# Last two products of a row-tile block set moved beside the next batch's products, one block sum a step, chunk 14 computed plainly

## The chip, the cores and the metric

The kernel runs on one NeuronCore of a Trainium2 chip. The metric is the device time of one execution in microseconds (us). Its engines are named as the profile names them: PE (TensorE, the matmuls), PEld (its weight loads), DVE (VectorE), ACT (ScalarE), POOL (GpSimd) and SP, which issues most of the DMAs.

## The reference

```python
attn_out = softmax(causal(q k^T / 8 + min(bias, 0))) v        # 2 x 8 heads, 576 x 64
x = attn_out as [1152, 512]
P = sinkhorn(exp(x @ w_gate), 8 rounds)                       # 1152 x 8
out = sum over e of P[:, e] * (relu(x @ w1[e]) @ w2[e])       # 8 experts, 512 -> 1024 -> 512
h = out @ w_in ; g = softplus(h) ; result = g @ w_out         # 512 -> 2048 -> 512
```

All products keep nearly full float32 precision: each factor is split into a high and a low part, and a product of two blocks is high x high, high x low and low x high, three matmuls for each 128 rows of contraction.

## The kernel before

After the attention, the work is cut into 20 chunks x of 512 hidden columns: chunks 0 to 15 are the eight experts (`NX` = 16, two chunks each), chunks 16 to 19 the last feed-forward (`NH` = 20). A chunk has an up side (x @ w1 with the activation) and a down side (the result @ w2, added to `acc`). Tokens are two batches g of 576 rows, each four row tiles of 128 and half of the fifth, middle tile (`NB` = 4).

**Up side.** `Unit` computes a batch's up side for one of two column halves a, b with a seven-product block scheme, products p1, p2, p6, p7, p5, p3, p4. Each is six matmuls with 288 moving columns (line 502). ACT and DVE evict the results.

**Down side.** Plain: `downs` does for each row tile four steps of three matmuls of 512 columns (line 578) and one DVE addition into `acc`. In the chunks that `SEVEN` lists (14, 17, 18 and 19), `pairs` replaces it: the four row tiles of a batch are two pairs (r = 0, 1), each a 2 x 2 block product done in seven products a11, s3, s2, a22, s1, s4, a12. One product of one pair is six matmuls of 256 columns (line 420) and a DVE addition `add_to` (lines 381, 384); 14 of these make one batch. The middle tile stays plain. The PSUM bank of a pair (`py`) holds all its products one after the other, and a product on a bank waits until the addition of the product before on the same bank has read it.

**What the block scheme needs ahead.** The up side's results go in full precision into `hw` (`evict`, `word`). `h_steps` makes from them the sums s3, s2, s1, s4 (POOL, line 334), the high parts (ACT, line 327) and the low parts (DVE, line 330; `hl`, `sl`; the middle tile's is the one of 128x256, name "m"). `prep_b` and `prep_t` make the blocks of w2 and their sums t1 to t4 for the next chunk (POOL line 256, ACT 243 and 226, DVE 245 and 228). w1's sums and splits are lines 161 to 170 (POOL), 152 (ACT) and 155 (DVE).

**Order.** It is written by hand: `play` walks a string. "a1" and the like are up products, "d" takes one step of the down side, "E", "F", "e" append a batch's block preparation to a list, "x", "y", "=" and "w" others; after each product or d, `step` advances every list by one. A chunk x plays two strings: the A string has the up products of (x, batch 1) beside the down side of (x, batch 0), the B string the up products of (x+1, batch 0) beside the middle tile and the down side of (x, batch 1). Before, the 14 steps of `pairs(x, 0)` all stand in A and those of `pairs(x, 1)`, behind four steps of the middle tile, all in B. After the last up product, the string for chunk 19's second batch has only down steps: the tail.

Of the kernel before, what the change touches and what calls it, by code (L numbers as in the profile page):

```python
# [20 lines left out]
def attention_moe_ffn(ctx, tc, q, k, v, s, w_gate, w1, w2, w_in, w_out, out):  # L21
# [107 lines left out]
    sp_t = {}  # L129
    SEVEN = (NX - 2, NX + 1, NX + 2, NX + 3)  # L130

# [190 lines left out]
    def h_steps(x, g, part):  # L322

        z = h_sets(g)

        def high(n):
            nc.scalar.activation(out=z[n][0], in_=z[n][2], func=AF.Copy)

        def low(n):
            nc.vector.tensor_tensor(out=z[n][1], in0=z[n][2], in1=f(z[n][0]), op=ALU.subtract)  # L330
            ready.add((x, g, n))

        def sum_(o, a, b, op):
            nc.gpsimd.tensor_tensor(out=z[o][2], in0=z[a][2], in1=z[b][2], op=op)

        if part == "e":
            hold((x, g), (None,))
            sum_("s3", "a11", "a21", ALU.subtract)
            high("a11")
            yield  # L340
            low("a11")
            yield
            last = (x - 1 + g, 1 - g)
            assert not seven(last[0]) or (*last, "done") in ready
            high("s3")
            yield
        elif part == "E":
            high("m")
            high("a22")
            yield  # L350
            low("s3")
            low("m")
            low("a22")
            sum_("s2", "a22", "s3", ALU.subtract)
            yield
            sum_("s1", "a21", "a22", ALU.add)
            yield
            high("a12")
            yield
            low("a12")  # L360
            high("s2")
            yield
            sum_("s4", "a12", "s2", ALU.subtract)
            high("s1")
            yield
            low("s2")
            low("s1")
            hold(None, ((x, g),))
            yield
        else:  # L370
            high("s4")
            yield
            low("s4")
            yield

    def add_to(x, t, cols, py, first, tile_col):
# [11 lines left out]

    def pairs(x, g, middle=None):

# [15 lines left out]
        for a, b, bank, start, tile_, col, first in (  # L406
# [4 lines left out]
            if a == "s3" and middle is not None:  # L411
                yield from middle
            for r in range(2):
# [8 lines left out]
                flush()  # L422
                if a == "s4" and r:
                    ready.add((x, g, "done"))
                add_to(x, rows_of(g) // P + 2 * r + tile_, d[col], o, first, (tile_, col))
# [60 lines left out]
    class Unit:  # L486
# [32 lines left out]
        def p2(self):  # L519
# [3 lines left out]
            nc.vector.tensor_tensor(out=b, in0=b, in1=self.v1, op=ALU.add)  # L523
            evict(self.x, 5 if seven(self.x) else 0, b, self.p, self.h0)

# [10 lines left out]
        def p5(self):  # L536
# [4 lines left out]
            defer(0, lambda: nc.vector.tensor_tensor(out=t, in0=self.c, in1=u4, op=ALU.add))  # L541
            evict(self.x, 1, t, self.p + 2, self.h1)

# [59 lines left out]
    with tc.manual_schedule():  # L603
# [685 lines left out]
        def play(seq, todo, d=None):  # L1289


            for z in seq.split():
# [14 lines left out]
                if z[0] in "eEF":  # L1307
                    g = int(z[1])
                    if seven(x if g else x + (z[0] == "e")):
                        side.append(h_steps(x if g else x + (z[0] == "e"), g, z[0]))  # L1310
                    continue
# [30 lines left out]
        for x in range(NH):  # L1342
# [101 lines left out]
```

## Time and profile before

| what | us |
|---|---|
| median of 3 runs (lowest, highest) | 1088.13 (1088.04, 1088.27) |
| profiled execution | 1089.59 |
| its span, first to last instruction | 1087.8 |
| PE busy | 1056.2 (97%) |
| DVE busy | 799.5 (73%) |
| ACT / POOL busy | 525.3 (48%) / 406.1 (37%) |
| granted TensorE clock, mean | 0.996 |

The 1.8 us between span and execution lie outside the instructions. A PE duration in a row is that of one pipelined matmul to its modelled end; what a matmul costs in a dense row is the distance of two starts. A chunk's stretch is read between two like places of neighbouring chunks.

### The profile page before, as it was taken

Reading aid. Unit: us, or ns where it says so; the run is one execution under the profiler, and the core shown is the slowest. Engines: PE = TensorE matmul, PEld = TensorE weight load, DVE = VectorE, ACT = ScalarE, POOL = GpSimd, SP = SyncE. Lnnn points to the kernel's source line nnn. Section 1 sums busy time; section 2 is a strip of 40 time slices with the busy share of each in tenths; the row PEclk is TensorE's granted clock in tenths of the full one; section 3 lists DMA queues with packets and bytes.
Section 4 is the critical chain, followed back from the end, with each engine's and each line's share of the span. In section 5 each row is a group of like instructions: output and inputs, shape, how many; then the busy total and the mean of one; then the engine's idle time right before and its main releaser. Section 6 shows DMA issues by size and latency. Waiting matters only on the chain.

```text
span 1087.8 us, 18435 instructions
## 1 busy us (share of the span) xinstructions
PE 1056.2 (97%) x6876; PEld 942.5 (87%) x6876; DVE 799.5 (73%) x1725; ACT 525.3 (48%) x1232; POOL 406.1 (37%) x449
## 2 busy tenths in 40 slices
PE   6999999999999999999999999999999999999987
PEld 4777888889888888988888898888899888898987
DVE  5576566667877878787887888775477487678876
ACT  6998544334443433434343343334454365555542
POOL 8885303053342414134241423423262233546321
PEclk9999999999999999999999999999999999999999
DMA  6221111122232222223222231311111011201002
GB/s 195 78 83 55 39 40 39 40 92 96 89 130 88 80 97 98 100 77 124 91 74 98 97 107 68 127 59 39 39 40 59 20 40 39 78 21 59 1 16 73
DMA packets 31538, 78.47 MB, mean 72 GB/s; under 512 B 5856, under 2 KB 13024, under 8 KB 31448
## 3 DMA queue, kind: packets, MB, share of 16 engines
q1 hardware_dynamic: 28704, 68.69, 18.9%
q0 software_dynamic: 2560, 8.39, 2.0%
q8 instruction: 54, 0.88, 0.3%
q14 instruction: 36, 0.29, 0.1%
q10 hardware_dynamic: 184, 0.20, 0.1%
HBM read 65.99 MB, written 10.75 MB: 71 GB/s over the span
## 4 chain that ended last, share of the span: by engine, by line
PE 82%; DVE 10%; ACT 3%; issue 2%; POOL 2%; DMA 0%; POOLq 0%; ACTq 0%; DVEq 0%
PE py L578 36%; PE ph L502 35%; PE py L420 5%; DVE hl L330 2%; PE sc L794 2%; POOL eb L857 1%; PE pv L901 1%; DVE sl L330 1%; PE tr L875 1%; DVE xl L1198 1%; DVE acc L381 1%; DVE xt L1229 1%; DVE ph L523 1%; PE sc L798 1%; DVE w1l L155 1%
## 5 line engine op out<-in xcount | busy, mean ns | idle before, releaser
L502 PE MATMUL ph<-xh,w1h 128*128 128x288 f32 x1120 | 331.7, 296 | 0.3 <-ACT v L510 0.3
L502 PE MATMUL ph<-xh,w1l 128*128 128x288 f32 x1120 | 330.8, 295 | 0.0
L502 PE MATMUL ph<-xl,w1h 128*128 128x288 f32 x1120 | 329.3, 294 | 0.0
L578 PE MATMUL py<-w2h,hh 128*128 128x512 f32 x588 | 233.5, 397 | 1.0 <-DVE acc L590 1.0
L578 PE MATMUL py<-w2l,hh 128*128 128x512 f32 x588 | 232.5, 395 | 0.2 <-POOL w2l L201 0.2
L578 PE MATMUL py<-w2h,hl 128*128 128x512 f32 x588 | 232.4, 395 | 0.0
L502 PEld LDWEIGHTS ph<-xh,w1h 128*128 128x128 f32 x1120 | 210.0, 188 | 18.4 <-ACT v L510 0.5
L502 PEld LDWEIGHTS ph<-xl,w1h 128*128 128x128 f32 x1120 | 210.4, 188 | 16.9
L502 PEld LDWEIGHTS ph<-xh,w1l 128*128 128x128 f32 x1120 | 210.3, 188 | 0.0
L510 ACT ACTIVATE v<-ph 128x288 f32<-128x288 f32 x160 | 64.0, 409 | 187.5 <-PE ph L502 184.8
L469 ACT ACTIVATE hh<-ph 128x288 fp32r<-128x288 f32 x180 | 73.7, 411 | 151.8 <-DVE ph L552 78.2
L578 PEld LDWEIGHTS py<-w2h,hl 128*128 128x128 f32 x588 | 110.5, 188 | 26.5
L201 POOL TENSOR_TENSOR w2l<-raw,w2h 128x512 fp32r<-128x512 f32 x36 | 51.3, 1427 | 215.9 <-ACT w2h L199 215.9
L596 DVE SCALAR_TENSOR_TENSOR acc<-py,gate,acc 128x512 f32<-128x512 f32 x118 | 88.0, 746 | 49.2 <-PE py L578 49.0
L1166 POOL TENSOR_TENSOR cm<-cm,ct 128x512 f32<-128x512 f32 x32 | 45.1, 1408 | 201.5 <-DVE ct L1164 201.5
L578 PEld LDWEIGHTS py<-w2h,hh 128*128 128x128 f32 x588 | 110.4, 188 | 10.5 <-DVE acc L590 1.2
L578 PEld LDWEIGHTS py<-w2l,hh 128*128 128x128 f32 x588 | 110.5, 188 | 10.0 <-POOL w2l L201 0.7
L155 DVE TENSOR_TENSOR w1l<-raw,w1h 128x512 fp32r<-128x512 f32 (+1 forms) x160 | 109.8, 686 | 11.3 <-ACT w1h L152 11.3
L476 DVE SCALAR_TENSOR_TENSOR hl<-ph,hh 128x288 fp32r<-128x288 f32 x180 | 81.2, 453 | 26.7 <-ACT hh L469 25.1
L152 ACT ACTIVATE w1h<-raw 128x512 fp32r<-128x512 f32 (+1 forms) x160 | 91.1, 571 | 0.0
L541 DVE TENSOR_TENSOR t<-ph,v 128x288 f32<-128x288 f32 x80 | 36.4, 455 | 54.5 <-ACT v L510 53.9
L510 ACT ACTIVATE u<-ph 128x288 f32<-128x288 f32 x80 | 32.7, 411 | 55.5 <-PE ph L502 53.4
(246 smaller groups left out, 1779.2 us busy)
## 6 DMA issues: line engine op xcount, KB each, us to landing
raw<-in_w SPq DMA_DIRECT2D x64, 512.0 KB
f<-in_w_in SPq DMA_DIRECT2D x16, 512.0 KB
f<-in_w_out SPq DMA_DIRECT2D x16, 512.0 KB
wd<-cm POOLq DMA_DIRECT2D x32, 256.0 KB, 3.1
raw<-wd SPq DMA_DIRECT2D x16, 512.0 KB
vv<-in_v SPq DMA_DIRECT2D x8, 256.0 KB
out<-acc SPq DMA_DIRECT2D x16, 128.0 KB
qk<-in_k SPq DMA_DIRECT2D x7, 288.0 KB
```

The costliest lines, as they stand in the source:

```text
L152: nc.scalar.activation(out=hi[:, o], in_=t[:, src], func=AF.Copy)
L155: nc.vector.tensor_tensor(out=lo[:, o], in0=t[:, src], in1=f(hi[:, o]), op=ALU.subtract)
L201: (nc.gpsimd if i else nc.vector).tensor_tensor(out=lo, in0=t[:, r], in1=f(hi), op=ALU.subtract)
L420: nc.tensor.matmul(o, u, v, start=(start and c == 0 and n == 0), stop=(c == 1 and n == 2), skip_group_check=True)
L469: nc.scalar.activation(out=hh, in_=z, func=AF.Relu)
L476: nc.vector.scalar_tensor_tensor(out=hl, in0=z, scalar=0.0, in1=f(hh), op0=ALU.max, op1=ALU.subtract)
L502: nc.tensor.matmul(o, u, v, start=(start and c == 0 and n == 0), stop=(c == 1 and n == 2), skip_group_check=True)
L510: nc.scalar.activation(out=t, in_=self.a, func=AF.Copy)
L541: defer(0, lambda: nc.vector.tensor_tensor(out=t, in0=self.c, in1=u4, op=ALU.add))
L578: nc.tensor.matmul(py[t], u, v, start=(k == 0 and n == 0), stop=(k == NF - 1 and n == 2))
L596: nc.vector.scalar_tensor_tensor(out=a, in0=py, scalar=gate_t[0][:, t, e:e + 1], in1=a, op0=ALU.mult, op1=ALU.add)
L1166: nc.gpsimd.tensor_tensor(out=m, in0=m, in1=f(t), op=ALU.add)
```

## The change

Four things: chunk 14 leaves `SEVEN`; A and B strings of the block chunks pair every up product with one d (two where the middle tile stands), so that the last four steps of a batch's 14 (s4 and a12, both pairs) fall beside the next batch's a1, b1, a2, b2; `h_steps` makes its sums and splits in 13 steps where it had 3 and 7, starting with the string and no longer before it; the words of p2 and p5 are written later (8 and 4 flushes instead of 5 and 1). In the tail, the last four steps of batch 0 come first and the middle tile's four steps (D) stand between down steps.

```diff
-    SEVEN = (NX - 2, NX + 1, NX + 2, NX + 3)
+    SEVEN = (NX + 1, NX + 2, NX + 3)
...
-        if part == "e":
-            hold((x, g), (None,))
-            sum_("s3", "a11", "a21", ALU.subtract)
-            high("a11")
-            yield
-            low("a11")
-            yield
...
-            high("s3")
-            yield
-        elif part == "E":
-            high("m")
-            high("a22")
-            yield
-            low("s3")
-            low("m")
-            low("a22")
-            sum_("s2", "a22", "s3", ALU.subtract)
-            yield
-            sum_("s1", "a21", "a22", ALU.add)
-            yield
...
+        if part == "F":
+            assert (x, g, "s3 done") in ready
             high("s4")
             yield
             low("s4")
             yield
+            return
+        hold((x, g), (None,))
+        sum_("s3", "a11", "a21", ALU.subtract)
+        high("m")
+        yield
+        high("a11")
+        low("m")
+        yield
+        high("a22")
+        low("a11")
+        yield
+        low("a22")
+        yield
...
+        high("s3")
+        yield
+        low("s3")
+        yield
+        sum_("s2", "a22", "s3", ALU.subtract)
+        yield
+        high("a12")
+        yield
+        sum_("s1", "a21", "a22", ALU.add)
+        yield
+        high("s2")
+        yield
+        low("s2")
+        yield
+        low("a12")
+        high("s1")
+        yield
+        sum_("s4", "a12", "s2", ALU.subtract)
+        low("s1")
+        hold(None, ((x, g),))
+        yield
...
-            evict(self.x, 5 if seven(self.x) else 0, b, self.p, self.h0)
+            evict(self.x, 8 if seven(self.x) else 0, b, self.p, self.h0)
...
-            evict(self.x, 1, t, self.p + 2, self.h1)
+            evict(self.x, 4 if seven(self.x) else 1, t, self.p + 2, self.h1)
...
-        A7_SEQ = "E0 a1 b1 a2 b2 =0 d d a6 d b6 d d F0 a7 d d b7 =1 d d a5 d b5 d d a3 d b3 e1 a4 d b4"
-        A7_LAST = "E0 a1 b1 a2 b2 d a6 d d b6 d d F0 a7 d d b7 d d a5 d b5 d a3 d b3 e1 a4 b4 d d"
-        B7_SEQ = ("E1 a1 b1 =2 a2 b2 d d d d a6 d d {11} b6 d d {3} F1 a7 d b7 d {2} a5 d b5 d {4} d a3 d {1} d b3 e0 d {22} a4 d b4 d {21}")
+        A7_SEQ = ("E0 a1 ~ b1 ~ {22} a2 ~ b2 ~ {21} =0 a6 d b6 d a7 d b7 d F0 =1 a5 d b5 d a3 d b3 d a4 d b4 d")
+        B7_SEQ = ("E1 a1 d b1 d a2 d b2 d =2 a6 d d b6 d d {12} a7 d d {11} b7 d d {3} F1 a5 d b5 d {2} a3 d b3 d {4} a4 d b4 d {1}")
...
+        LAST = "E1 d d D d D d D D d d d d F1 " + "d " * 10
...
+                d = then(d if seven(x - 1) else (), pairs(x, 0))
+                play(seq, products(x, 1), d)
...
+                    d = then(d, downs(x, [(NB,)]), pairs(x, 1))
...
-                    play("E1 n n n n " + "d " * 8 + "F1 " + "d " * 10, {}, pairs(x, 1, downs(x, [(NB,)], "tr")))
+                    middle = downs(x, [(NB,)], "tr")
+                    play(LAST, {"D": lambda: next(middle)}, then(d, pairs(x, 1)))
```

"~" is a d where the chunk before was a block chunk too, and nothing in chunk 17.

**DVE around the middle tile in chunk 17's B string, before.** The row of `acc<-py` with 512 columns is the middle tile's addition; `hl` and `sl` rows are low parts, `w1l` w1's, `ph` rows up products, `acc` with 256 columns one block product's addition:

```order
L381 TENSOR_TENSOR acc<-py,acc 128x256
L330 TENSOR_TENSOR hl<-hw,hh 128x2x2x128
L552 TENSOR_TENSOR ph<-ph,u 128x288
L330 TENSOR_TENSOR sl<-xw,sh 128x512
L330 TENSOR_TENSOR hl<-hw,hh 128x4x64
L330 TENSOR_TENSOR hl<-hw,hh 128x2x2x128
L523 TENSOR_TENSOR ph<-ph,v 128x288 x2
L155 TENSOR_TENSOR w1l_10580<-raw_10106,w1h_10579 128x256
L330 TENSOR_TENSOR hl<-hw,hh 128x2x2x128
L330 TENSOR_TENSOR sl<-xw,sh 128x512
L330 TENSOR_TENSOR hl<-hw,hh 128x2x2x128
L593 TENSOR_TENSOR acc<-py,acc 128x512
```

The same place after:

```order
L330 TENSOR_TENSOR hl<-hw,hh 128x2x2x128
L384 TENSOR_TENSOR acc<-py,acc 128x256
L330 TENSOR_TENSOR hl<-hw,hh 128x2x2x128
L524 TENSOR_TENSOR ph<-ph,v 128x288
L384 TENSOR_TENSOR acc<-py,acc 128x256
L330 TENSOR_TENSOR sl<-xw,sh 128x512
L524 TENSOR_TENSOR ph<-ph,v 128x288
L384 TENSOR_TENSOR acc<-py,acc 128x256
L155 TENSOR_TENSOR w1l_10463<-raw_9972,w1h_10462 128x256
L330 TENSOR_TENSOR sl<-xw,sh 128x512
L330 TENSOR_TENSOR hl<-hw,hh 128x2x2x128 x2
L594 TENSOR_TENSOR acc<-py,acc 128x512
```

The additions of s4 and a12 of the batch before now stand between the low parts; the four rows right ahead of the middle tile's addition are the same work as before.

**DVE in the tail, before,** from the last up products (L552) to the middle tile's addition (`pyt`):

```order
L552 TENSOR_TENSOR ph<-ph,u 128x288 x2
L330 TENSOR_TENSOR hl<-hw,hh 128x2x2x128
L381 TENSOR_TENSOR acc<-py,acc 128x256 x2
L330 TENSOR_TENSOR sl<-xw,sh 128x512
L330 TENSOR_TENSOR hl<-hw,hh 128x4x64
L330 TENSOR_TENSOR hl<-hw,hh 128x2x2x128
L381 TENSOR_TENSOR acc<-py,acc 128x256
L330 TENSOR_TENSOR hl<-hw,hh 128x2x2x128
L381 TENSOR_TENSOR acc<-py,acc 128x256
L330 TENSOR_TENSOR sl<-xw,sh 128x512
L330 TENSOR_TENSOR hl<-hw,hh 128x2x2x128
L593 TENSOR_TENSOR acc<-pyt,acc 128x512
```

The same place after:

```order
L553 TENSOR_TENSOR ph<-ph,u 128x288
L384 TENSOR_TENSOR acc<-py,acc 128x256 x3
L330 TENSOR_TENSOR hl<-hw,hh 128x4x64
L330 TENSOR_TENSOR hl<-hw,hh 128x2x2x128
L384 TENSOR_TENSOR acc<-py,acc 128x256
L330 TENSOR_TENSOR hl<-hw,hh 128x2x2x128
L384 TENSOR_TENSOR acc<-py,acc 128x256
L330 TENSOR_TENSOR sl<-xw,sh 128x512
L594 TENSOR_TENSOR acc<-pyt,acc 128x512
L384 TENSOR_TENSOR acc<-py,acc 128x256 x3
L330 TENSOR_TENSOR sl<-xw,sh 128x512
```

The middle tile's low part (128x4x64) now stands behind three additions, and the low parts of a12, s2 and s1 no longer stand ahead of the middle tile's addition.

## Rows read from the trace of the kernel before

**Rows 1.** Stretches: us, busy of PE, PEld, DVE, ACT, POOL, clock, DMA.

```profile
734.16:781.64 47.48, 47.48 (x277) 42.56 (x277) 24.73 (x48) 18.49 (x43) 12.25 (x13) 1.00 0.13 45
953.84:1004.11 50.27, 46.33 (x350) 44.60 (x350) 42.12 (x74) 27.19 (x60) 24.38 (x21) 1.00 0.13 43
1004.11:1054.58 50.47, 46.32 (x350) 44.63 (x350) 42.03 (x73) 26.27 (x58) 20.77 (x17) 1.00 0.00 1
```

**Rows 2.** Timeline of PE, chunk 17: start, duration, first matmuls of five steps.

```profile
961.02 0.29 PE L502 MATMUL ph<-xh,w1h 128*128 128x288 f32 x1
...
961.82 0.28 PE L420 MATMUL py<-w2h,hh 128*128 128x256 f32 x1
...
962.52 0.29 PE L502 MATMUL ph<-xh,w1h 128*128 128x288 f32 x1
...
968.80 0.39 PE L578 MATMUL py<-w2h,hh 128*128 128x512 f32 x1
...
970.20 0.39 PE L578 MATMUL py<-w2h,hh 128*128 128x512 f32 x1
```

**Rows 3.** PE's waits from 940 to 1065 us: total, times, longest.

```profile
PE py L420 <- DVE acc L381: 6.0, 9, 1.1
PE py L420 <- DVE acc L593: 2.7, 2, 1.3
PE py L420 <- ACT w1h L152: 1.1, 1, 1.1
```

**Rows 4.** Pieces of the chain that ended last, chunks 13 and 15.

```profile
748.32 1.40 PE py L578 x6
...
845.23 1.40 PE py L578 x6
```

**Rows 5.** Timeline around the middle tile's addition in chunk 17.

```profile
971.73 1.67 POOL L334 TENSOR_TENSOR hw<-hw,xw 128x512 f32<-128x512 f32 x1 [0.96 <-DVE hl L330]
...
972.18 1.78 DVE L330 TENSOR_TENSOR hl<-hw,hh 128x512 fp32r<-128x512 f32 x1
...
973.88 0.68 DVE L593 TENSOR_TENSOR acc<-py,acc 128x512 f32<-128x512 f32 x1
...
974.61 0.39 PE L420 MATMUL py<-w2h,hh 128*128 128x256 f32 x1 [1.34 <-DVE acc L593]
```

**Rows 6.** Timeline around the low part of t3 in chunk 17.

```profile
982.49 1.73 POOL L256 TENSOR_TENSOR xw<-raw,raw 128x512 f32<-128x512 f32 x1
...
983.33 1.43 DVE L245 TENSOR_TENSOR tl<-raw,th 128x512 fp32r<-128x512 f32 x1
...
985.05 0.41 DVE L381 TENSOR_TENSOR acc<-py,acc 128x256 f32<-128x256 f32 x1
...
985.52 0.38 PE L420 MATMUL py<-th,hh 128*128 128x256 f32 x1 [1.08 <-DVE acc L381]
```

**Rows 7.** Groups of 953.84 to 1054.58: count, busy us, mean ns, idle before.

```profile
L381 DVE TENSOR_TENSOR acc<-py,acc 128x256 f32<-128x256 f32 x56 | 23.0, 417 | 7.7 <-PE py L420 7.4
L330 DVE TENSOR_TENSOR hl<-hw,hh 128x512 fp32r<-128x512 f32 x16 | 16.5, 1033 | 0.0
```

```profile
L334 POOL TENSOR_TENSOR xw<-hw,xw 128x512 f32<-128x512 f32 x4 | 5.3, 1324 | 10.7 <-ACT hh L327 7.1 <-DVE sl L330 3.7
...
L168 POOL TENSOR_TENSOR raw<-raw 128x256 f32<-128x256 f32 x4 | 2.9, 737 | 1.4 <-DVE w1l L155 1.4
```

**Rows 8.** One low part with no POOL work beside it, chunk 17.

```profile
965.35 0.68 DVE L330 TENSOR_TENSOR hl<-hw,hh 128x512 fp32r<-128x512 f32 x1
```

**Rows 9.** The tail: timeline of PE, then a stretch with its clock.

```profile
1064.92 0.28 PE L420 MATMUL py<-w2h,hh 128*128 128x256 f32 x1
...
1075.16 0.36 PE L420 MATMUL py<-th,sh 128*128 128x256 f32 x1 [2.23 <-DVE acc L381]
...
1084.04 0.28 PE L420 MATMUL py<-w2h,hl 128*128 128x256 f32 x1
```

```profile
1076.60:1080.00 3.40, 3.40 (x18) 3.40 (x18) 1.87 (x4) 0.00 (x0) 0.00 (x0) 0.51 0.11 38
```

More of the change, by code (lines that the diff above doesn't have):

```diff
@@ L334, in sum_ @@
             nc.gpsimd.tensor_tensor(out=z[o][2], in0=z[a][2], in1=z[b][2], op=op)
-        if part == "e":
-            hold((x, g), (None,))
-            sum_("s3", "a11", "a21", ALU.subtract)
-            high("a11")
-            yield
-            low("a11")
-            yield
-            last = (x - 1 + g, 1 - g)
-            assert not seven(last[0]) or (*last, "done") in ready
-            high("s3")
-            yield
-        elif part == "E":
-            high("m")
-            high("a22")
-            yield
-            low("s3")
-            low("m")
-            low("a22")
-            sum_("s2", "a22", "s3", ALU.subtract)
-            yield
-            sum_("s1", "a21", "a22", ALU.add)
-            yield
[L358 to L370, printed above, removed]
+        if part == "F":
+            assert (x, g, "s3 done") in ready
             high("s4")
@@ L374, in h_steps @@
             yield
+            return
[11 more added lines that the diff above has]
+        yield
+        last = (x - 1 + g, 1 - g)
+        assert not seven(last[0]) or (*last, "s4 done") in ready
+        high("s3")
[19 more added lines that the diff above has]
+        yield
     def add_to(x, t, cols, py, first, tile_col):
@@ L387, in add_to, with pairs @@
             nc.sync.dma_start(out=out[t * P:(t + 1) * P, cols], in_=a)
-    def pairs(x, g, middle=None):
+    def pairs(x, g):
         z = h_sets(g)
@@ L410, in pairs @@
                 ("a12", "b21", 1, True, 0, 0, False)):
-            if a == "s3" and middle is not None:
-                yield from middle
             for r in range(2):
@@ L422, in pairs @@
                 flush()
-                if a == "s4" and r:
-                    ready.add((x, g, "done"))
+                if r:
+                    ready.add((x, g, a + " done"))
                 add_to(x, rows_of(g) // P + 2 * r + tile_, d[col], o, first, (tile_, col))
@@ L1306, in play @@
                     continue
[L1307 to L1310, printed above, removed]
+                if z[0] in "EF":
+                    side.append(h_steps(x, int(z[1]), z[0]))
+                    continue
+                if z[0] == "X":
+                    bot.append(prep_b(x, z[1:]))
                     continue
@@ L1323, in attention_moe_ffn @@
         TURN = ("t0 d d d d u0 d d d d d a1 d b1 d a2 d =2 b2 t1 d a6 d b6 d a7 d b7 d a5 d b5 d d u1 w0 a3 w2 b3 w1 a4 w3 b4")
-        A7_SEQ = "E0 a1 b1 a2 b2 =0 d d a6 d b6 d d F0 a7 d d b7 =1 d d a5 d b5 d d a3 d b3 e1 a4 d b4"
-        A7_LAST = "E0 a1 b1 a2 b2 d a6 d d b6 d d F0 a7 d d b7 d d a5 d b5 d a3 d b3 e1 a4 b4 d d"
-        B7_SEQ = ("E1 a1 b1 =2 a2 b2 d d d d a6 d d {11} b6 d d {3} F1 a7 d b7 d {2} a5 d b5 d {4} d a3 d {1} d b3 e0 d {22} a4 d b4 d {21}")
-        TO_SEVEN = B_SEQ.replace("b2", "b2 y3 y2 y4 y1").replace("b3", "b3 e0")
-        B7 = {True: {"11": "x11 x12 y0", "3": "y3", "2": "y2", "4": "y4", "1": "y1", "22": "x22", "21": "x21"},
-              False: {"11": "w0 w1", "3": "", "2": "", "4": "", "1": "", "22": "", "21": "w2 w3"}}
+        A7_SEQ = ("E0 a1 ~ b1 ~ {22} a2 ~ b2 ~ {21} =0 a6 d b6 d a7 d b7 d F0 =1 a5 d b5 d a3 d b3 d a4 d b4 d")
+        B7_SEQ = ("E1 a1 d b1 d a2 d b2 d =2 a6 d d b6 d d {12} a7 d d {11} b7 d d {3} F1 a5 d b5 d {2} a3 d b3 d {4} a4 d b4 d {1}")
+        TO_SEVEN = B_SEQ.replace("b2", "b2 y3 y2 y4 y1")
+        B7 = {True: {"12": "x12", "11": "x11 y0", "3": "y3", "2": "y2", "4": "y4", "1": "y1"},
+              False: {"12": "", "11": "w0 w1", "3": "", "2": "", "4": "", "1": "d d d d w2 w3"}}
+        A7 = {True: {"~": "d", "{22}": "X22", "{21}": "X21"}, False: {"~": "", "{22}": "", "{21}": ""}}
+        LAST = "E1 d d D d D d D D d d d d F1 " + "d " * 10
         A_GROUPS = [(0, 1), (2,), (3,)]
@@ L1351, in attention_moe_ffn @@
             if seven(x):
-                play(A7_SEQ if x + 1 < NH else A7_LAST, products(x, 1), pairs(x, 0))
+                seq = A7_SEQ
+                for k, z in A7[seven(x - 1)].items():
+                    seq = seq.replace(k, z)
+                d = then(d if seven(x - 1) else (), pairs(x, 0))
+                play(seq, products(x, 1), d)
             else:
@@ L1366, in attention_moe_ffn @@
                         seq = seq.replace("{" + k + "}", z)
-                    play(seq, products(x + 1, 0), then(downs(x, [(NB,)]), pairs(x, 1)))
+                    play(seq, products(x + 1, 0), d)
                 else:
-                    play("E1 n n n n " + "d " * 8 + "F1 " + "d " * 10, {}, pairs(x, 1, downs(x, [(NB,)], "tr")))
+                    middle = downs(x, [(NB,)], "tr")
+                    play(LAST, {"D": lambda: next(middle)}, then(d, pairs(x, 1)))
                 if not seven(x + 1):
```

## The prediction

> **What bounds the kernel now.** I read the stretches first [rows 1]: in a plain chunk PE is busy for all of its 47.48 us, so nothing but matmuls sets the pace there. In a block chunk PE is idle: 50.27 and 50.47 us for fewer columns. The timeline of PE gives the prices [rows 2]: an up product (six matmuls of 288) takes 961.82 - 961.02 = 0.80 us, a block step (six of 256) 962.52 - 961.82 = 0.70, three of 512 (970.20 - 968.80) / 2 = 0.70. A block chunk has 28 up products, 28 block steps and 4 middle steps: 28 x 0.80 + 32 x 0.70 = 44.8 us. So 5.5 us of each block period are no matmul work. The list of PE's waits says what ended them [rows 3]: between 940 and 1065 us twelve waits, 6.0 + 2.7 + 1.1 = 9.8 us, nearly all for a DVE addition. The list counts from the modelled end of a matmul of 0.28 us, while the next would have started after 0.12, so each wait costs 0.16 more: 9.8 + 12 x 0.16 = 11.7 us. The tail has one of 2.2 [rows 9].
>
> Why DVE is late is seen in two places. Around the middle tile [rows 5] a low part starts at 972.18 and takes 1.78 us; alone such a row takes 0.68 [rows 8]. It ends 0.56 us after the POOL sum that runs from 971.73 to 973.40. So it stood still until POOL had finished. Behind it, at 973.88, comes the middle tile's addition, and PE, whose bank it frees, resumes at 974.61. At t3 [rows 6] it is the same: the POOL sum ends at 984.22, the low part at 984.76, and the addition that PE waits for starts at 985.05. Over two periods the low parts of 512 average 1033 ns, the additions, which read PSUM and one tile in SBUF, 417 [rows 7]. DVE is therefore not full (42.1 of 50.3 us [rows 1]); it is an in-order queue in which additions stand behind low parts that POOL holds up.
>
> **The change, part by part.**
> Chunk 14 plain. From a place in chunk 13 to the same place in chunk 15 the chain takes 845.23 - 748.32 = 96.91 us [rows 4]; two plain chunks take 94.96 [rows 1]. Chunk 14 costs 1.95 us more as blocks than plain, although it saves 12 matmuls of 512 (2.8 us): its stalls and the rest eat that and more. Plain, it is one more of a kind that keeps PE busy throughout [rows 1]. Gain **1.95 us**; its preparation on POOL, DVE and ACT goes with it at no further price, since PE sets the pace.
>
> Strings of chunks 17 to 19. Matmuls are the same in number. What moves is the distance between two products on one bank: before, in "d d a6 d d", a bank's next product came 0.70 to 1.50 us after the last (one block step, with or without an up product); now there is an up product, the other pair's step and an up product between them, 0.80 + 0.70 + 0.80 = 2.30 us, except in the four places of B with two d in a row, 1.50 us. An addition needs some 0.16 for the last matmul's end and 0.42 [rows 7], so DVE may now lag by about 1.7 us, or 0.9, before PE stops. No wait is added; the additions of s4 and a12 are now queued beside the first low parts of the next batch. I take each kind of stall in turn, with 0.6 us of DVE time for a low part alone and the rest of the POOL sum where one has just started.
> - Middle tile (2 x 1.5 us): the same four DVE rows stand ahead of its addition, but its last matmul now comes about 10.4 us into the string instead of 6.0, while the low parts start where they did. They are through by 10.2, the addition ends at 11.2, its bank is wanted at 11.9. Kept: 0.
> - t3's low part (1.6 us in each of two B strings: the wait of 1.08 in [rows 6] with its 0.16, and a small one ahead of it): t3 still needs two POOL sums on w2's raw blocks, which wait for the low parts of these blocks, some 15 us into the string, and its low part then meets the third sum. s2's addition for the second pair is queued behind it: wanted at 20.1 us, done at about 21.5. Kept: 1.4 each, 2.8 in all; bounds 0 and 1.6 each.
> - A strings (the rest of the 11.7, 5.5 us in three strings): the sums s2 and s1 and four of w1's meet low parts of w2, s2, a12, s1 and w1 on DVE; each takes a POOL sum of 0.7 to 1.3 us [rows 7] and 0.57 of its own, five of them some 7 us, and four additions 1.4, against 7 us of PE from the first of them to the bank that they block. Chunk 18 keeps 1.0; chunk 17, where w1's sums come earlier, 0.4; chunk 19, which has none, 0.3. Kept: 1.7; bounds 0 and 5.5.
> So 11.7 us fall to 4.5: gain **7.2 us**, bounds 11.7 and 3.0 (all of t3 and A kept).
>
> The block sums spread over 13 steps cost nothing by themselves: each has the same POOL, ACT and DVE work. The product s3 comes 9.8 us into an A string, in chunk 17 7.0, and its sum and parts take some 1.3, 0.6 and 0.6 of it, so I put nothing on the head start that is gone. The later words hold p2's bank until the seventh product, where nothing asks for it.
>
> Tail. From the last up product's end, 1064.92, to the last matmul, 1084.04 + 0.12, are 19.24 us [rows 9] for 16 block steps and 4 middle steps: 14.1. Excess 5.1: the wait of 2.2 with its 0.16, two small ones of 0.65, 15 matmuls at a granted clock of 0.51 (from 1076.60 on, after PE had done almost nothing from 1072.9 to 1075.16), 0.21 instead of 0.12 each, 1.4 in all, and some 0.5 of a bank chain too tight at 0.70. After, there are two more block steps here and two fewer before. The first middle step starts 1.4 us in and wants the middle tile's low part, which stands behind s4's second addition: done at 2.4, so 0.5 lost. Later a12's and s1's low parts stand between additions with s4's POOL sum beside them: 1.2 lost at a22; the chain at the end 0.3. Kept 2.0, gain **3.1 us**; bounds 4.6 (only the chain is kept) and 1.5 (the low clock comes back). No wait there reaches the 2.2 us that came before the low clock; after the 1.34 us wait [rows 5] the clock stayed at 1.00 through the stretch [rows 1].
>
> Sum: 1.95 + 7.2 + 3.1 = 12.2 us. The profiled execution, 1089.59 (span 1087.8 and 1.8 around it), would come to 1077.4; it ran 1.46 above the median, and against the median 1088.13 - 12.2 = **1075.9 us**. Half-way to the bounds on either side, the forecast's own range is 1073 to 1079.
>
> **The rivals.**
> The slack swallows everything: additions that are 2.3 us away from their bank's next use never hold PE, and the t3 chain is shorter than I walk it. Kept are 1 us in the strings and 1 in the tail: 1.95 + 10.7 + 4.1 = 16.8, 1071.3 us. For it: no addition in the trace is itself slow. Against: DVE would have 42.1 us to do in about 45.5.
> The stalls move: with 7 us fewer per period DVE has no idle time in which to catch up, and lags pile up from string to string. If some 10 us of the 11.7 stay, the gain is 1.95 + 1.7 + 3.1 = 6.7, 1081.4 us. For it: in both rows where a low part met a POOL sum, it lost the whole rest of it [rows 5, 6].
> The slower end: POOL holds DVE in nearly every step. POOL is busy 24.4 and 20.8 us in a period [rows 1]; now DVE loses some 6.7 (16 low parts of 512 lose 0.35 each in two periods [rows 7, 8], and other low parts like them more than as much again: an estimate). Were every POOL microsecond, 22.6 on average, one of DVE's, DVE would need 42.1 + 15.9 = 58 us a period, 7.6 more than now: over 2.5 periods 19 us, less 1.95 and 3.1, 1102 us. It decides from 52.4 us of DVE a period on, where the gains elsewhere are used up. Against: DVE alternates with POOL, and a third of its rows, the additions, are untouched.
> The Trainium skill has a rule for this, in SBUF — State Buffer, Who interferes with whom: a DVE instruction with two SBUF inputs and a GpSimd one that reads SBUF exclude each other for the whole of the one that came first. The two meetings above agree with it, and by it every further meeting of a sum and a low part, which one sum a step invites, is paid in full, as in this rival.
>
> **How the numbers follow.** Forecast 0.55; all swallowed 0.24; stalls moved 0.17; slower 0.04. The range must hold 0.8: 1070.5 takes in most of the first rival, 1080.5 leaves out the last and most of the third. A measurement of this kernel tells 0.2%, 2.2 us, from no change. Faster by more 0.95, within 0.01, slower 0.04.
>
> **What would show it.** The span from chunk 13 to 15 should be 94.96 us. PE's waits for the middle tile's addition (2.7 us) should be gone, one wait near a22 in each B string left, behind t3's low part; periods of the block chunks near 48 us; in the tail a wait of the first middle step's third matmul and a clock at 1.00 throughout. I am wrong if PE waits for a low or high part of a block (operands late, not banks), or if additions start late with no POOL sum beside the low part ahead.

## The result and the profile after

The changed kernel takes 1078.72 us (median of 4 runs, 1077.75 to 1078.83) against 1088.09 us in the same runs: ratio 0.9912, 95% interval 0.9895 to 0.9929, 9.4 us faster where 12.2 were forecast. Its profiled execution took 1078.83 us, with a span of 1077.0, against 1089.59 before. Single executions of either kernel differ by a microsecond or more, for a reason that the last section shows.

The stretches of the changed kernel, columns as in [rows 1]: chunk 13 to 15, then the strings A17, B17, A18, B18, A19 (each from its first up product to the next string's) and the tail. Lines 384, 421, 579 and 594 are the earlier 381, 420, 578 and 593.

```profile
747.81:842.77 94.96, 94.96 (x554) 85.11 (x553) 48.50 (x94) 36.23 (x81) 16.85 (x20) 1.00 0.14 45
...
939.84:959.69 19.85, 19.05 (x146) 18.41 (x145) 16.27 (x28) 11.27 (x27) 16.02 (x14) 1.00 0.17 54
959.69:985.72 26.03, 24.56 (x183) 23.43 (x181) 21.41 (x39) 13.41 (x31) 9.79 (x7) 1.00 0.12 42
985.72:1007.69 21.97, 21.50 (x170) 21.06 (x169) 19.75 (x35) 13.01 (x30) 15.44 (x13) 1.00 0.14 49
1007.69:1034.00 26.31, 24.55 (x183) 23.43 (x181) 21.72 (x39) 13.42 (x31) 9.79 (x7) 1.00 0.00 1
1034.00:1054.29 20.29, 20.29 (x164) 20.29 (x163) 15.73 (x31) 11.02 (x26) 7.60 (x5) 1.00 0.04 14
1054.29:1077.00 22.71, 17.84 (x128) 16.16 (x126) 14.42 (x29) 4.81 (x9) 3.87 (x3) 1.00 0.27 93
```

Chunks 13 and 14 are now two plain chunks, 94.96 us; the clock is 1.00 in the tail, where in the profile of before it was 0.51 for 3.4 us [rows 9]. A19 has no idle PE left; B17 and B18 still have 1.5 and 1.8 us of it, counted from modelled ends. The list of PE's waits from 940 to 1077 us (total, times, longest), beside [rows 3]:

```profile
PE py L421 <- DVE acc L384: 3.7, 6, 1.0
PE py L421 <- DVE acc L594: 1.4, 2, 0.8
PE pyt L579 <- DVE hl L330: 0.4, 1, 0.4
PE py L421 <- DVE sl L330: 0.3, 1, 0.3
```

[rows 3] ends ahead of the tail. Up to there 9.8 us of waits became 4.4, and in the tail 2.5 became 1.4, which makes the 5.8 of this list. Three places hold most of what is left. First the middle tile's addition in B17 (timeline, all engines):

```profile
968.89 0.41 ACT L511 ACTIVATE u<-ph 128x288 f32<-128x288 f32 x1 [0.96 <-PE ph L503]
...
969.19 0.62 ACT L152 ACTIVATE w1h<-raw 128x512 fp32r<-128x512 f32 x1
...
969.72 0.62 ACT L327 ACTIVATE hh<-hw 128x512 fp32r<-128x512 f32 x1
...
969.79 1.30 POOL L334 TENSOR_TENSOR hw<-hw,xw 128x512 f32<-128x512 f32 x1 [1.63 <-DVE hl L330]
...
970.37 1.27 DVE L330 TENSOR_TENSOR hl<-hw,hh 128x512 fp32r<-128x512 f32 x1 [0.72 <-ACT hh L327]
...
971.56 0.68 DVE L594 TENSOR_TENSOR acc<-py,acc 128x512 f32<-128x512 f32 x1
...
972.29 0.39 PE L421 MATMUL py<-w2h,hh 128*128 128x256 f32 x1 [0.55 <-DVE acc L594]
```

DVE is idle for 0.72 us ahead of s1's low part, because ACT makes its high part (`hh`, 969.72) only after the copy `u`, which waits for an up product, and a high part of w1. Then the low part meets the POOL sum s4 and takes 1.27, where alone it takes 0.68 [rows 8]. The second place is t3's low part (`tl`) in B17, where [rows 6] were before:

```profile
978.87 1.74 POOL L256 TENSOR_TENSOR xw<-raw,raw 128x512 f32<-128x512 f32 x1
...
979.61 1.55 DVE L245 TENSOR_TENSOR tl<-raw,th 128x512 fp32r<-128x512 f32 x1
...
981.45 0.74 DVE L384 TENSOR_TENSOR acc<-py,acc 128x256 f32<-128x256 f32 x2
...
981.91 0.39 PE L421 MATMUL py<-th,hh 128*128 128x256 f32 x1 [0.92 <-DVE acc L384]
```

The third is the tail: the middle tile's low part behind an addition, then s1's low part beside the sum s4:

```profile
1056.70 0.42 DVE L384 TENSOR_TENSOR acc<-py,acc 128x256 f32<-128x256 f32 x1 [0.36 <-PE py L421]
...
1057.04 0.41 DVE L330 TENSOR_TENSOR hl<-hw,hh 128x256 fp32r<-128x256 f32 x1
...
1057.51 0.50 PE L579 MATMUL pyt<-w2h,hl 128*128 128x512 f32 x1 [0.39 <-DVE hl L330]
...
1065.90 1.28 POOL L334 TENSOR_TENSOR hw<-hw,xw 128x512 f32<-128x512 f32 x1 [1.99 <-DVE hl L330]
...
1066.01 1.72 DVE L330 TENSOR_TENSOR hl<-hw,hh 128x512 fp32r<-128x512 f32 x1
...
1067.66 0.74 DVE L384 TENSOR_TENSOR acc<-py,acc 128x256 f32<-128x256 f32 x2
...
1068.12 0.38 PE L421 MATMUL py<-th,hh 128*128 128x256 f32 x1 [1.00 <-DVE acc L384]
```

### The profile page after: what moved, and what is told of

It reads as the page before. It is cut to its first block, busy times and chain, and to the rows that moved or that the text cites. A ratio compares the mean times of both kernels' runs of the same rounds, so it can differ in the third digit from the quotient of the medians.

```text
span 1077.0 us, 18208 instructions
## 1 busy us (share of the span) xinstructions
PE 1055.4 (98%) x6804; PEld 938.7 (87%) x6804; DVE 777.2 (72%) x1701; ACT 513.9 (48%) x1212; POOL 389.1 (36%) x437
## 4 chain that ended last, share of the span: by engine, by line
PE 87%; DVE 5%; POOL 3%; issue 2%; ACT 2%; DMA 0%; POOLq 0%; ACTq 0%; DVEq 0%; SPq 0%
PE py L579 39%; PE ph L503 38%; PE py L421 4%; PE sc L795 1%; PE pv L902 1%; PE tr L876 1%; DVE xl L1199 1%; POOL hw L334 1%; POOL eb L858 1%; DVE xt L1230 1%; ACT eb L845 1%; POOL raw L256 1%; PE tr L870 0%; PE sc L799 0%; DVE acc L384 0%
## 5 line engine op out<-in xcount | busy, mean ns | idle before, releaser
L579 PE MATMUL py<-w2h,hh 128*128 128x512 f32 x620 | 246.2, 397 | 1.0 <-DVE acc L591 1.0
L579 PE MATMUL py<-w2l,hh 128*128 128x512 f32 x620 | 245.1, 395 | 0.2 <-POOL w2l L201 0.2
L579 PE MATMUL py<-w2h,hl 128*128 128x512 f32 x620 | 245.1, 395 | 0.0
L470 ACT ACTIVATE hh<-ph 128x288 fp32r<-128x288 f32 x192 | 78.5, 411 | 160.0 <-DVE ph L553 80.7
L579 PEld LDWEIGHTS py<-w2h,hl 128*128 128x128 f32 x620 | 116.5, 188 | 27.9
L597 DVE SCALAR_TENSOR_TENSOR acc<-py,gate,acc 128x512 f32<-128x512 f32 x126 | 93.9, 745 | 56.2 <-PE py L579 56.0
L579 PEld LDWEIGHTS py<-w2h,hh 128*128 128x128 f32 x620 | 116.4, 188 | 10.8 <-DVE acc L591 1.2
L579 PEld LDWEIGHTS py<-w2l,hh 128*128 128x128 f32 x620 | 116.6, 188 | 10.4 <-POOL w2l L201 0.7
L477 DVE SCALAR_TENSOR_TENSOR hl<-ph,hh 128x288 fp32r<-128x288 f32 x192 | 86.4, 452 | 31.2 <-ACT hh L470 29.5
```

The source lines that it names most:

```text
L470: nc.scalar.activation(out=hh, in_=z, func=AF.Relu)
L477: nc.vector.scalar_tensor_tensor(out=hl, in0=z, scalar=0.0, in1=f(hh), op0=ALU.max, op1=ALU.subtract)
L579: nc.tensor.matmul(py[t], u, v, start=(k == 0 and n == 0), stop=(k == NF - 1 and n == 2))
L597: nc.vector.scalar_tensor_tensor(out=a, in0=py, scalar=gate_t[0][:, t, e:e + 1], in1=a, op0=ALU.mult, op1=ALU.add)
```

## The experiments

Timed runs of one kernel differ by up to 3.6 us (chunk 14 plain alone: 1084.90 to 1088.47 in ten; before: 1086.82 to 1089.17 in thirteen); what the traces show of the cause stands in the last section. Plain chunks agree to 0.02 us between profiles, and strings of the same code to 0.1 us, with one exception of 0.3: B18 takes 26.31 in the changed kernel and 26.02 in the run c14_blocks, whose strings from A17 on are the same. So the kernels are compared by string, in us from the first up product to the next string's, in their profiles; "tail" ends with the end of the last matmul, and so does the last row. The runs that name the columns are described below.

| string | before | after | packed2 | bundled | s1_early | t2_on_dve | sums_on_dve | combo | best |
|---|---|---|---|---|---|---|---|---|---|
| A17 | 23.31 | 19.85 | 22.01 | 19.49 | 19.67 | 19.83 | 18.90 | 19.66 | 18.89 |
| B17 | 27.42 | 26.03 | 26.28 | 25.46 | 25.21 | 25.19 | 25.45 | 24.36 | 24.36 |
| A18 | 22.84 | 21.97 | 24.09 | 23.35 | 21.99 | 22.08 | 22.18 | 21.98 | 22.09 |
| B18 | 27.42 | 26.31 | 26.32 | 25.47 | 25.22 | 25.18 | 25.45 | 24.36 | 24.36 |
| A19 | 21.63 | 20.29 | 22.64 | 22.13 | 20.29 | 20.30 | 20.40 | 20.30 | 20.30 |
| tail | 19.40 | 19.28 | 18.49 | 20.57 | 19.27 | 19.27 | 19.16 | 19.29 | 17.65 |
| chunk 13 to last matmul | 341.55 | 331.31 | 337.40 | 334.03 | 329.23 | 329.46 | 329.16 | 327.55 | 325.26 |

The counts of steps differ in a few cells: A17 has four down steps fewer after than before (2.8 us), A19 one more (0.7), the tail three more (2.1); in packed2 A19 has one more than after and the tail one less.

**Chunk 14 plain, alone.** The kernel before with one line changed.

```diff
-    SEVEN = (NX - 2, NX + 1, NX + 2, NX + 3)
+    SEVEN = (NX + 1, NX + 2, NX + 3)
```

> The kernel before with one part of the change alone: chunk 14 leaves SEVEN, the strings and the block preparation stay as they were. Theory (the parts are independent, the term of 1.95 us is right): 1088.1 - 1.95 = 1086.1 us, and the span from chunk 13 to chunk 15 is 94.96 us. Rival (chunk 14's blocks also delayed what follows it, w2's preparation or chunk 15's): more than 2.5 us gained, below 1085.6.

The timed ratio is 0.9991 (0.9981 to 1.0), medians 1087.35 and 1088.12: 0.8 us. The trace gives the 1.95 exactly, 94.96 us from chunk 13 to 15; all strings from A17 on agree with those of before to 0.02 us, so nothing else is lost or won:

```profile
748.08:843.04 94.96, 94.96 (x553) 85.12 (x553) 48.53 (x94) 36.26 (x81) 16.87 (x20) 1.00 0.13 45
```

The rest is scatter of the granted clock: among runs with the same mean clock the edit is worth what the trace says. At 1.000 the kernel before took 1086.82 to 1087.01 us in four runs and this one 1084.90 in one; at 0.998 1087.97 to 1088.54 in eight and 1085.90 and 1086.03 in two. The term stands; the two medians alone could not have shown it.

**Chunk 14 as blocks, in the new strings.** The same line, the other way, in the changed kernel.

```diff
-    SEVEN = (NX + 1, NX + 2, NX + 3)
+    SEVEN = (NX - 2, NX + 1, NX + 2, NX + 3)
```

> The changed kernel with chunk 14 put back into SEVEN, now with the new strings. Theory (blocks lose more in stalls than they save in matmuls under the new strings too): a block chunk has 44.8 us of matmul work, and by the stretches of chunk 17 in the changed kernel about 1.7 us of stall in its A string and 2.2 in its B string, 48.7 in all against 47.48 plain: 1.2 us slower than the changed kernel, 1079.9 us. Rival (without softplus the stalls of chunk 14 vanish): 2.7 us faster, 1076.0 us.

1078.10 us median (1077.80 to 1079.04), 0.6 below the changed kernel; but A14 and B14 together take 47.81 us against 47.48, so the chunk costs 0.33 more as blocks. B18 is 0.29 shorter, though its code is the same, and chunk 13 starts 0.8 us earlier in this profile. Neither theory's size held. With the new strings chunk 14 is almost an even trade: plain, it is worth 0.33 us beside the rest of the change, not the 1.95 of before.

**All chunks plain.** The changed kernel without blocks.

```diff
-    SEVEN = (NX + 1, NX + 2, NX + 3)
+    SEVEN = ()
```

> The changed kernel with SEVEN empty: chunks 17 to 19 are plain too. Theory (PE sets the pace of a plain chunk throughout): from the first up product of chunk 17's second batch 70 up products of 0.80 and 108 down steps of 0.70 are 131.6 us and a tail of about 1 us, against 137.2 us in the changed kernel: 4.5 us faster, about 1074 us. Rival (softplus, which costs ACT two passes for each product of a plain chunk, holds up PE there): PE waits for ACT in chunks 18 and 19, and the time is above 1078.7 us.

1076.33 us median, 2.4 below the changed kernel; from chunk 13 to the end of the span 333.15 us against 334.74, 1.6 less, and chunk 13 starts 0.8 earlier. PE waits for nothing from 939 us on, and ACT is half idle, so the rival on softplus falls (two chunks, the last strings, the tail):

```profile
939.06:986.54 47.48, 47.48 (x278) 42.56 (x277) 23.49 (x48) 23.49 (x57) 8.43 (x10) 1.00 0.14 45
986.54:1034.02 47.48, 47.48 (x278) 42.56 (x277) 23.50 (x48) 23.48 (x57) 8.42 (x10) 1.00 0.08 23
1034.02:1054.96 20.94, 20.94 (x128) 19.02 (x127) 8.61 (x18) 8.63 (x23) 1.30 (x1) 1.00 0.10 38
1054.96:1074.60 19.64, 15.56 (x68) 12.19 (x66) 5.35 (x9) 0.85 (x3) 0.00 (x0) 0.98 0.22 81
```

The matmuls take 131.46 us, as worked out. My 4.5 was too much: I had put the end of the plain tail at 1 us, and from the last matmul to the end of the span it is 4.1. What matters: in the changed kernel too, the block scheme of chunks 17 to 19 loses more in stalls than its fewer matmuls save.

**Distance between two products on a bank.** The strings of the changed kernel with the down steps two by two behind one up product; packed2 has w2's block 22 set as the changed kernel does.

```diff
-A7_SEQ = ("E0 a1 ~ b1 ~ {22} a2 ~ b2 ~ {21} =0 a6 d b6 d a7 d b7 d F0 =1 a5 d b5 d a3 d b3 d a4 d b4 d")
+A7_SEQ = ("E0 a1 b1 a2 ~ ~ {22} b2 ~ ~ {21} =0 a6 d d b6 d d F0 a7 d d b7 =1 d d a5 d d b5 a3 b3 a4 b4")
-B7_SEQ = ("E1 a1 d b1 d a2 d b2 d =2 a6 d d b6 d d {12} a7 d d {11} b7 d d {3} F1 a5 d b5 d {2} a3 d b3 d {4} a4 d b4 d {1}")
+B7_SEQ = ("E1 a1 b1 a2 d d b2 d d =2 a6 d d b6 d d {12} a7 d d {11} b7 d d {3} F1 a5 d d {2} b5 d d {4} a3 d d {1} b3 a4 b4")
```

> The changed kernel with the same steps in each string, but the down steps put two by two behind one up product in the middle of the string, and the first and last up products alone, so that a product comes 1.50 us after the last one on its bank and no longer 2.30. The block preparation stays one step at a time and the last four steps of a batch stay beside the next batch's products. Theory (the distance on a bank is what removed the stalls of the strings): about 1.3 us come back in each of the five strings, 1084 to 1086 us, as waits for DVE additions. Rival (carrying four steps over and spreading the sums did it): within 1 us of the changed kernel, below 1079.8 us.

> As the run called packed (the down steps two by two behind one up product, a product 1.50 us after the last one on its bank), but with w2's block 22 of the next chunk put in place behind the last product that reads the old one, as the changed kernel has it. Compared by its strings in the trace. Theory (distance on a bank is what removed the strings' stalls): strings about 1.3 us longer each than in the changed kernel, A18 near 23.3 and B17 near 27.3, some 1084 to 1086 us. Rival (carrying four steps over and the spread sums did it): each string within 0.3 us of the changed kernel's, below 1080 us.

In the run packed, w2's block 22 of the next chunk overwrites the old one ahead of the product s4 that still has to read it, so its output is computed from a wrong block; it took 1093.13 us, 7.0 of it in A18, and tells nothing on the distance. packed2 took 1084.46 us, inside the 1084 to 1086 of the theory, but not as the theory said: for the same steps A17 became longer by 2.2 us, A18 by 2.1 and A19 by 1.7, and the B strings by no more than 0.3. PE's waits in packed2:

```profile
PE py L421 <- DVE acc L384: 4.9, 10, 1.0
PE py L421 <- DVE sl L330: 1.7, 1, 1.7
PE py L421 <- DVE acc L594: 1.4, 2, 0.7
PE py L421 <- ACT w1h L152: 1.0, 1, 1.0
```

In A18 and A19 the added waits are for additions, as the theory wants. In A17 they are for s2's low part (1.74) and for w1's high part (0.96): there the product comes before its operand. So the edit cost some 3.8 us in A18 and A19, and the distance is the reading that fits; but it moves the products against the preparation too, and no run separates the two. The B strings owe the distance next to nothing.

**Preparation bundled.** The second half of `h_steps` with the order and the bundles of before, strings unchanged.

```diff
         low("s3")
-        yield
         sum_("s2", "a22", "s3", ALU.subtract)
-        yield
-        high("a12")
-        yield
         sum_("s1", "a21", "a22", ALU.add)
         yield
-        high("s2")
-        yield
-        low("s2")
+        high("a12")
         yield
         low("a12")
+        high("s2")
+        yield
+        sum_("s4", "a12", "s2", ALU.subtract)
         high("s1")
         yield
-        sum_("s4", "a12", "s2", ALU.subtract)
+        low("s2")
         low("s1")
```

> The changed kernel with the second half of the block preparation bundled as before: the sums s2 and s1 in one step together with s3's low part, then high and low parts two to a step, 10 steps in place of 13. Theory (the prediction's: spreading the sums costs and gains nothing by itself, since each engine runs what it is given as soon as its operands are there): every string within 0.4 us of the changed kernel's. Rival (one sum a step is what keeps POOL from holding DVE ahead of additions): A and B strings 0.5 to 1 us longer each, 3 to 5 us in all.

1081.54 us, 2.7 more than the changed kernel from chunk 13 to the last matmul: A18 1.4, A19 1.8 and the tail 1.3 longer, but B17 0.6, B18 0.8 and A17 0.4 shorter. Neither theory: how the preparation is spread matters, with different signs in different strings. In A18 two low parts in a row are held (1.00 and 1.75 us), and two additions stand behind them:

```profile
995.33 1.00 DVE L330 TENSOR_TENSOR hl<-hw,hh 128x512 fp32r<-128x512 f32 x1
...
995.74 1.72 POOL L334 TENSOR_TENSOR hw<-hw,xw 128x512 f32<-128x512 f32 x1
...
996.26 1.75 DVE L228 TENSOR_TENSOR w2l<-raw,w2h 128x512 fp32r<-128x512 f32 x1
...
997.93 0.74 DVE L381 TENSOR_TENSOR acc<-py,acc 128x256 f32<-128x256 f32 x2
...
998.40 0.39 PE L418 MATMUL py<-th,sh 128*128 128x256 f32 x1 [2.08 <-DVE acc L381]
```

**The middle tile's wait.** s1's high part one step earlier on ACT.

```diff
         low("s2")
+        high("s1")
         yield
         low("a12")
-        high("s1")
         yield
```

> The changed kernel with one edit: the high part of s1 on ACT is issued one step earlier, ahead of the up product's copy. Theory (the middle tile's two waits, 0.70 and 0.99 us, come from s1's low part on DVE, which waits for its high part behind that copy in ACT's queue and then meets the POOL sum s4): both waits go, B17 26.0 becomes 25.3 and B18 26.3 becomes 25.3, 1.7 us in all. Rival (DVE's load alone makes it late; the time lost comes back at the next bank): the strings stay within 0.3 us.

1076.19 us; B17 is 0.82 us shorter and B18 1.09 (0.80 by c14_blocks, as said above), and both waits for L594 are gone. The high part starts at 966.90, as soon as POOL has made its sum, and the two low parts run as one pair without a pause:

```profile
966.90 0.63 ACT L327 ACTIVATE hh<-hw 128x512 fp32r<-128x512 f32 x1 [0.27 <-POOL hw L334]
...
967.68 1.28 DVE L330 TENSOR_TENSOR hl<-hw,hh 128x512 fp32r<-128x512 f32 x2
...
968.50 1.62 POOL L334 TENSOR_TENSOR hw<-hw,xw 128x512 f32<-128x512 f32 x1 [1.63 <-DVE hl L330]
...
968.99 0.69 DVE L594 TENSOR_TENSOR acc<-py,acc 128x512 f32<-128x512 f32 x1
```

Now POOL's s4 comes second and is the one that waits (1.62 in place of 1.30); the middle tile's addition beside it takes its usual 0.69. The order in ACT's queue was the cause.

**t3's low part.** The sum for t2 on DVE.

```diff
-                sum_(w, b["22"], b["11"])
+                nc.vector.tensor_tensor(out=w, in0=b["22"], in1=b["11"], op=ALU.subtract)
```

> The changed kernel with the sum for t2 made on DVE, behind t3's low part and the addition that PE waits for, and no longer on POOL beside that low part. Theory (POOL holds the low part: 1.55 us where alone it takes 0.68): the low part falls to about 0.7 and the wait at a22 from 1.08 to about 0.2 in both B strings, 1.7 us in all. Rival (DVE is simply full there; the sum's own 0.68 us takes the place of the lost 0.87): a wait of at least 0.8 stays near a22 or appears one product later, and B17 and B18 stay within 0.4 us.

1075.85 us; B17 is 0.84 us shorter and B18 1.13; at a22 0.23 us stays of 1.08. A18 has one wait of 0.62 in place of two of 0.24 and 0.23, but so has c14_blocks without this edit, so that no lag is shown to have moved there. The low part takes 0.69 in place of 1.55, and the sum follows the addition that PE needs:

```profile
978.52 0.69 DVE L245 TENSOR_TENSOR tl<-raw,th 128x512 fp32r<-128x512 f32 x1 [0.15 <-ACT th L243]
...
979.50 0.41 DVE L384 TENSOR_TENSOR acc<-py,acc 128x256 f32<-128x256 f32 x1
...
979.83 0.68 DVE L275 TENSOR_TENSOR xw<-raw,raw 128x512 f32<-128x512 f32 x1
...
979.97 0.39 PE L421 MATMUL py<-th,hh 128*128 128x256 f32 x1
```

**All block sums on DVE.** `sum_` of `h_steps`.

```diff
-            nc.gpsimd.tensor_tensor(out=z[o][2], in0=z[a][2], in1=z[b][2], op=op)
+            nc.vector.tensor_tensor(out=z[o][2], in0=z[a][2], in1=z[b][2], op=op)
```

> The changed kernel with all four block sums of a batch (s3, s2, s1, s4) made on DVE and no longer on POOL. Theory (POOL's sums cost DVE about as much in held low parts as they would cost on DVE itself): low parts in the block preparation fall to 0.68 us, DVE's busy time in the stretches stays within 1.5 us, and A and B strings change by less than 0.7 us each. Rival 1 (DVE's work is the limit): 4 x 0.68 = 2.7 us more on DVE in each string, strings 1 to 2 us longer. Rival 2 (holding costs much more than the sum, because additions queue behind it): strings 0.7 to 1.5 us shorter.

1075.72 us; A17 is 0.95 us shorter, B17 0.58, B18 0.86, A18 and A19 0.2 and 0.1 longer. Strings A17 and A18:

```profile
938.74:957.64 18.90, 18.74 (x146) 18.27 (x145) 17.49 (x32) 11.45 (x28) 9.45 (x9) 1.00 0.18 56
...
983.09:1005.27 22.18, 21.60 (x171) 21.11 (x169) 20.27 (x39) 13.12 (x31) 6.50 (x8) 1.00 0.14 48
```

In A17 DVE got four sums more and is busy 17.5 us in place of 16.3, 1.2 more for 2.7 of added work: the other 1.5 had been standing still for POOL, which was busy for 16.0 of 19.9. The first theory holds on DVE's busy time, which grows by 0.5 to 1.2 us a string; but A17 and B18 gain more than its 0.7 and so bear out rival 2, that additions queue behind the held rows. Rival 1 falls.

**Together.** combo has the edits of s1_early and t2_on_dve. best adds: sums on DVE in A17 alone, and in the tail the middle tile's low part one addition earlier and s4's sum on DVE behind s1's low part. best14 has chunk 14 as blocks again.

```diff
-            nc.gpsimd.tensor_tensor(out=z[o][2], in0=z[a][2], in1=z[b][2], op=op)
+            e = nc.vector if g == 0 and not seven(x - 1) or last_s4 and o == "s4" else nc.gpsimd
+            e.tensor_tensor(out=z[o][2], in0=z[a][2], in1=z[b][2], op=op)
...
-LAST = "E1 d d D d D d D D d d d d F1 " + "d " * 10
+LAST = "E1 n d d D d D d D D d d d d F1 " + "d " * 10
```

> The changed kernel with both edits that helped alone: s1's high part one step earlier on ACT, and the sum for t2 on DVE. Theory (the two waits of a B string have different causes in different places, so the gains add): B17 and B18, 25.2 us with either edit, fall to about 24.4; with an undisturbed start about 1073.5 us. Rival (both edits give DVE the same slack, and the lag is only moved): B17 and B18 stay at 25.0 or above, about 1075.5 us.

> As combo, and in addition: chunk 17's first batch makes its four block sums on DVE, where w1's sums fill POOL; in the tail the middle tile's low part is issued one addition earlier, and the sum s4 is made on DVE behind s1's low part. Theory: A17 falls from 19.8 to 18.9 us as it did with all sums on DVE; in the tail the wait of the first middle step (0.55) and most of the one at a22 (1.16) go, 19.3 becomes about 18.1; in all about 2.0 us below combo, 1071.5 us. Rival (the tail is bound by the chain of additions at 0.70 us a step): the tail stays above 18.8, 1072.5 us.

> As best, with chunk 14 in SEVEN again. Theory (with the stalls gone, blocks pay there too): its two strings, 47.8 us with the changed kernel's strings, lose the middle tile's wait of 0.84 and some 0.9 of its A string: about 46.1 against 47.48 plain, 1.4 us below best, about 1070.1 us. Rival (the gated additions and the evictions of plain chunk 15 keep DVE late): 47.5 or more, no gain on best.

combo: 1075.16 us (1074.11 to 1075.57), both B strings 24.36. In B17 the two gains add, 1.67 us against 0.82 and 0.84; in B18 1.95 against 1.09 and 1.13, which is the 0.3 that the changed kernel's B18 has too much. best: 1071.81 us (1071.53 to 1071.85); the tail fell to 17.65, more than forecast, and the rival of the tail's chain falls. best14: 1070.82 us (1070.09 to 1071.51), ratio to the kernel before 0.9843 (0.9827 to 0.9859), 7.9 us below the changed kernel; chunk 14 now takes 46.00 us as blocks:

```profile
788.66:834.66 46.00, 45.66 (x350) 44.55 (x349) 40.62 (x81) 25.38 (x58) 14.90 (x13) 1.00 0.17 58
```

The same chunk cost 1.95 us more than plain before the change, 0.33 more with its strings and 1.48 less here. best14 is also 5.5 us faster than all_plain, where the changed kernel was 2.4 slower: it hangs on the order in the queues whether blocks are worth having.

## Why the prediction was right, and where it was not

The forecast of a gain and its range held; the time came out 2.8 us above. 2.0 of it stand in the traces: from chunk 13 to the last matmul 12.25 us were forecast and 10.24 came, and two terms of the sum are short by that. The other 0.8 is what the sum was taken from. Its terms were read from a profile 1.46 us above the median, with the clock at about 0.5 for 3.4 us twice, at the start (18.6 to 22.0) and in the tail [rows 9]; the profile of after has it at the start alone. A run at the median of before, with a mean clock of 0.998, has room for one such stretch and not for both, and which one is not on record; four of the thirteen later runs, at 1.000, had neither. So the 1.4 us of low clock in the tail are a gain only in the executions that have it. Between runs at 1.000 the change is worth 9.2 us (1086.8 to 1087.0 in those four, 1077.75 in one of after).

- **Chunk 14**: 1.95 forecast, 1.95 measured in the trace of the change and of the edit alone. Its reason, that PE sets the pace of a plain chunk, held in all_plain too.
- **Strings**: 7.2 forecast, 6.1 measured for the same steps. By the prices of 0.80 and 0.70, the stall kept is 1.65 in A17 (0.4 forecast), 0.97 in A18 (1.0), none in A19 (0.3), 2.23 and 2.51 in the B strings (1.4 each): 7.4 and not 4.5. The gain missed by less, and by luck: the same prices give 13.4 us of stall in the five strings before, where the list of waits, in which a stall of under 0.16 us cannot show, had given 11.7. The step that failed is the middle tile, "Kept: 0": 0.70 and 0.99 us stayed. I had walked DVE's queue and let the low parts be through by 10.2 us and the addition by 11.2. They were through at 11.9 and 12.5, because s1's high part stands on ACT behind a copy that waits for PE; s1_early showed it by moving that one instruction. A17's miss was POOL's: w1's sums and the block sums hold DVE there, and sums_on_dve took 0.95 us of the 1.65 away. It held an operand up as well (PE waits for `sl` 0.3), which I had named as a sign of being wrong.
- **t3**: 1.4 us each forecast, 1.08 measured at the place named, and t2_on_dve confirmed the cause. The Trainium skill (SBUF — State Buffer, Who interferes with whom) says that a DVE instruction with two SBUF inputs and a GpSimd one that reads SBUF exclude each other for the whole of the first; this trace agrees, 1.55 against 0.69 us for the same row with and without the sum beside it, and in s1_early, where the DVE rows came first, POOL's sum took 1.62 in place of 1.30.
- **The mechanism**: I gave the distance on a bank as the reason for all strings. packed2 bears it out for A18 and A19, where undoing it cost more (2.1 and 1.7) than the whole change had gained for the same steps (0.9 and 2.0). The B strings kept nearly all of their gain at the old distance, and bundled made them shorter, so theirs is from elsewhere. The four steps carried over are left. The traces of B17 fit: PE wants the middle tile's bank 11.9 us into the string where it was 7.5, and the addition ends at 12.5 where it was 8.9, which is 0.8 of the 1.4 us gained. This was not tried by itself.
- **The spread sums**, at which I put nothing: undoing the second half of the spreading cost 2.7 us net. "Each has the same POOL, ACT and DVE work" was true and beside the point; which row stands ahead of an addition is what counts.
- **Tail**: 3.1 forecast, 2.2 measured between the two profiles: 19.12 us for 23 steps of 0.70, an excess of 3.0 where 2.0 was to stay. The two waits named are there with their sizes, 0.55 (0.5) and 1.16 (1.2), and no low clock. The chain at the end took 0.4 (0.3); some 0.9 are gaps of under 0.2 us that I had not counted.
- **The rivals**: the stalls did not move as a whole, nor was all swallowed. POOL did not hold DVE in nearly every step: the five strings together became shorter.

## What to carry to other kernels

When an engine is a queue of short urgent work behind longer work that another engine can hold up, look first at the order in the queues that feed it: one instruction moved on ACT and one sum a chunk moved from POOL to DVE gave 3.8 us here, where the whole change gave 10.2 in the same stretch of the trace. A transformation that saves matmuls is worth only what its stalls leave: price it against the plain form by the length of the stretch, again after each change, since its sign turned from +1.95 to -1.48 us here. And walk every queue that leads to a waited-for row, not only the row's own.

## What the runs showed of the hardware

The first 30 us vary from execution to execution. In five of the fourteen profiles (before, chunk 14 plain alone, the changed kernel, packed2, bundled) the granted clock of TensorE is at its half level, 1.2 of 2.4 GHz, for some 3.4 us between 16.8 and 22.0 us, and chunk 13 begins at 742.1 to 742.8 us. In the other nine it is not, and chunk 13 begins at 741.1 to 741.5, with the same code up to there. The stretch of the profile of before, then 10 to 20 us of the changed kernel and of all_plain:

```profile
18.60:22.00 3.40, 3.40 (x18) 2.58 (x20) 0.60 (x5) 3.04 (x10) 3.40 (x5) 0.50 0.98 374
```

```profile
10.00:20.00 10.00, 7.60 (x43) 4.76 (x42) 5.46 (x31) 7.27 (x21) 9.46 (x24) 0.84 0.60 189
```

```profile
10.00:20.00 10.00, 8.41 (x50) 4.77 (x50) 6.04 (x31) 8.33 (x25) 9.40 (x25) 1.00 0.58 179
```

Ahead of it PE stood idle twice, for POOL: 1.36 and 1.01 us in the changed kernel, 0.59 and 1.01 in before, 0.31 and 1.01 in all_plain, where the clock stayed at 1.00. What decides is not shown. The 1.1 us or so that such a stretch costs is more than several of the effects studied, so they were read from the traces.
